# The last matrix product of a retention and MoE kernel: a part of its tokens by Strassen's seven products

## The chip, the cores and the metric

The kernel runs on one core of one Trainium2 chip. Its time is the device time of one execution in microseconds (us), the median of three runs. Before the change it is 807.72 us (807.5 to 809.23).

## The reference

A retention layer (attention with a decay in place of a softmax), then two feed-forward layers, over 4 x 576 = 2304 tokens:

```
ret = (q k^T * scale * decay) v            # 4 batches, 8 heads, 576 positions, 64 wide
h   = ((x w1) * (x w2)) w3 w_out           # 2304 x 512, inner width 1024
g   = max(x w_in, 0) + alpha * min(x w_in, 0)   # 2304 x 2048
out = g w_out2                             # 2304 x 512
```

The change is in the last line alone: `g` (2304 x 2048) times `w_out2` (2048 x 512). The weights come as float64 and are converted on the core.

## The kernel before

Every number is held as the sum of two float32r parts, a high and a low one (`h`, `l`), and each product of two such numbers is three matmuls: h*h, h*l, l*h. ACT makes the high part with a copy, DVE the low part with a subtraction (`split`, lines 172 and 173).

The work goes through stages, most of them bound by TensorE: retention, the two products `a` and `b` (`ab_unit`), the folding of w3 and w_out into one matrix, `y`, and then `g`, which is already made with Strassen's seven products (class `Group`, 3 pairs of token blocks times 8 groups `j` of 256 columns of `g`). Each finished piece of `g` (128 columns of `g` by 384 tokens) is written to DRAM (`keep`, `gd`), since only a part fits on the core.

The output stage (lines 1015 to 1035) reads `g` back. It goes in 48 steps. A step is one `j` (256 rows of `w_out2`, in two chunks of 128) for one block `b` of 384 tokens, and has 3 token tiles x 2 chunks x 3 = 18 matmuls of 128x128 by 128x512, which accumulate in one bank of PSUM for each token tile. The first 16 steps take blocks 0 and 1 by turns for each `j` (6 of the 8 banks); the other 32 take one block after the other. `load_g(n + 3)` loads a step's `g` three steps ahead, `split_g(n + 1)` splits it one step ahead. `ghl` has two buffers, so ACT's copy for step n + 1 waits until PE has ended step n - 1.

Beside these steps the 16 chunks of `w_out2` are converted from float64 (class `Weights`). One `ws.tick()` moves a pipeline of four stages by one piece: ACT reads the raw bits (lines 93, 94), DVE puts a float32 together with four operations (lines 103 to 108), ACT makes the high part (112), DVE the low part (116). A piece is done four ticks after it began, and all 16 take 19 ticks. Six of these ticks stand in the last pair's groups (from `j >= 2`, line 1000), the others in the first 13 steps. The loads of raw weights have three buffers: SP issues the load of a piece only once DVE's line 106 has freed a buffer, and every load behind it in SP's queue waits too.

PE, ACT and SP run their instructions in the order in which the program makes them. DVE's order is set by the compiler's planner, which takes the instruction that is ready by its own estimate, with the earlier one in the program ahead of the later.

`tmp` holds the working tiles of the conversion: three buffers with the tag "a", two with the tag "b". `wa`, `hold` and `xo` hold split operands; `bank(i, ...)` gives one of the eight PSUM banks.

Of the kernel before, what the change touches and what calls it, by code (L numbers as in the profile page):

```python
# [16 lines left out]
P = 128  # L17
B, H, S, D = 4, 8, 576, 64
NPAIR = H // 2
NT, DM, DF1, DF2 = B * S, 512, 1024, 2048  # L20
# [3 lines left out]
C1 = DF1 // P  # L24
# [3 lines left out]
W = 384  # L28
NB = NT // W
# [3 lines left out]
def _f32(ap):  # L33
    return ap.bitcast(F32)
# [5 lines left out]
class Steps:  # L40
# [97 lines left out]
def retention_moe_kernel(ctx: ExitStack, tc, qk, kv, w_out1, w3t, w12, w_in, w_out2, alpha, c_row, c_pair, out):  # L138
    nc = tc.nc

    def pool(stack, name, bufs=1, **kw):
        return stack.enter_context(tc.tile_pool(name=name, bufs=bufs, **kw))
# [4 lines left out]
    raws = pool(ctx, "raws", bufs=3, side="left")  # L147
    tmp = pool(ctx, "tmp", bufs=2, side="left")
# [34 lines left out]
    wac, wo, w3p, wpc, wic, wbc = {}, {}, {}, {}, {}, {}  # L183
# [453 lines left out]
    xo = pool(ctx, "xo", bufs=8, side="left", reuse_waits="tile")  # L637
# [109 lines left out]
    def x_operands(p):  # L747

        x = xs_of[p]
        src = {"B11": x[:, 0:2, 0], "B21": x[:, 2:4, 0], "B22": x[:, 2:4, 1]}  # L750
        b12 = x[:, 0:2, 1]
        room_of = lambda m: a_sum(f"t{p}_{m}")[:, :2 * W].rearrange("p (k n) -> p k n", k=2)

        def hi(op):
            t = xop[p, op] = xo.tile([P, 2, 2, W], F32R, tag="xo", name=f"x{op}_{p}")
            nc.scalar.copy(t[:, 0], src[op])

        def lo(op):
# [33 lines left out]
    def x_room(p):  # L792
        xs_of[p] = xs2.tile([P, KT, 2, W], F32, tag="xs", name=f"xs2_{p}")
# [58 lines left out]
    gd = {}  # L852
# [69 lines left out]
            self.from_sum(self.b3, self.u2, 0, 1)  # L922

    NM = W // P
    steps = [(j, b) for j in range(C1) for b in range(2)] + [(j, b) for b in range(2, NB) for j in range(C1)]
    loaded, ready, accs = {}, {}, {}

    def load_g(n):
        if n < len(steps):
            j, b = steps[n]  # L930
            t = loaded[n] = gr.tile([P, 2, W], F32, tag="gr", name=f"gr{n}")
            for m in range(2):
                nc.sync.dma_start(out=t[:, m], in_=gd[2 * j + m, b])

    def split_g(n):
        if n < len(steps):
            x = loaded.pop(n)
            ready[n] = tuple(ghl.tile([P, 2, W], F32R, tag=f"g{m}", name=f"g{m}{n}") for m in "hl")
# [14 lines left out]
    def some_of(steps, n):  # L953
        for _ in range(min(n, len(steps))):
            steps.pop(0)()

    for n, (p, j) in enumerate(groups):
        last, first = j == C1 - 1 and p + 1 < NP, j == 0 and p > 0
        g = Group(p, j, n)
        flush()  # L960
        g.p1()
        g.p5()
        if last:
            some_of(make, 1)
# [12 lines left out]
        if before:  # L977
            before.p4()
            if first:
                some_of(make, 2)  # L980
                if p + 1 < NP:
                    x_room(p + 1)
                    for o in range(KT):
                        for t in range(2):
                            nc.sync.dma_start(out=xs_of[p + 1][:, o, t], in_=x2d[2 * (p + 1) + t, o])
                else:
                    pt.close()
                    gr = pool(ctx, "gr", side="left", bufs=3, reuse_waits="tile")
# [23 lines left out]
    flush()  # L1012


    pg.close()
    used = 0
    for n, (j, b) in enumerate(steps):
        if ws.at[3] < len(ws.pieces):
            ws.tick()
            ws.until(n_in + 2 * j + 2)  # L1020
        load_g(n + 3)
        split_g(n + 1)
        if b not in accs:
            accs[b] = [bank((used + i) % 8, f"o{b}_{i}") for i in range(NM)]
            used += NM
        h, l = ready.pop(n)
        for i in range(NM):
            ic = slice(i * P, (i + 1) * P)
            for m in range(2):
                wh, wl = wbc[2 * j + m]  # L1030
                for q, (x, y) in enumerate(((h, wh), (h, wl), (l, wh))):
                    nc.tensor.matmul(accs[b][i], x[:, m, ic], y, start=(j == 0 and m == 0 and q == 0),  # L1032
                                     stop=(j == C1 - 1 and m == 1 and q == 2))
            if j == C1 - 1:
                write(b, i)


# [79 lines left out]
```

## Time and profile before

| what | us |
|---|---|
| median of three runs | 807.72 |
| the profiled execution's own time | 808.39 |
| its span, first to last instruction | 806.6 |
| PE busy in the span | 788.3 |
| first matmul of the output stage starts | 604.41 |
| last matmul of the output stage starts | 802.40 |

The profiled execution is 0.67 us above the median, and 1.79 us of it lie outside the span. Matmuls are pipelined: one takes some 0.39 us from its start to its modelled end, and the next starts well before that. The cost of a matmul in a full stream is therefore the distance between two starts, and the same goes for DVE and ACT, where an instruction that needs nothing of the one before it starts a little ahead of its end.

### The profile page before, as it was taken

Reading aid. Unit: us, or ns where it says so; the run is one execution under the profiler, and the core shown is the slowest. Engines: PE = TensorE matmul, PEld = TensorE weight load, DVE = VectorE, ACT = ScalarE, POOL = GpSimd, SP = SyncE. Lnnn points to the kernel's source line nnn. Section 1 sums busy time; section 2 is a strip of 40 time slices with the busy share of each in tenths; the row PEclk is TensorE's granted clock in tenths of the full one; section 3 lists DMA queues with packets and bytes.
Section 4 is the critical chain, followed back from the end, with each engine's and each line's share of the span. In section 5 each row is a group of like instructions: output and inputs, shape, how many; then the busy total and the mean of one; then the engine's idle time right before and its main releaser. Section 6 shows DMA issues by size and latency. Waiting matters only on the chain.

```text
span 806.6 us, 12689 instructions
## 1 busy us (share of the span) xinstructions
PE 788.3 (98%) x4768; PEld 695.3 (86%) x4768; DVE 498.9 (62%) x895; ACT 349.4 (43%) x648; POOL 0.2 (0%) x4
## 2 busy tenths in 40 slices
PE   7889999999999999999999999999999999999998
PEld 4668888888888988999999999999997888888886
DVE  4786686425477689988852578677889923222222
ACT  3452472231245465655534455465566622222121
POOL 0000000000000000000000000000000000000000
PEclk9989999999999999999999999999999999999999
DMA  9833951391166568999925925325557635344341
GB/s 349 312 129 103 330 205 80 105 281 79 55 212 204 183 211 312 304 375 407 394 99 192 363 105 186 118 98 196 177 199 243 220 98 176 105 131 137 98 137 40
DMA packets 80765, 156.24 MB, mean 194 GB/s; under 512 B 9280, under 2 KB 57408, under 8 KB 80704
## 3 DMA queue, kind: packets, MB, share of 16 engines
q1 hardware_dynamic: 80704, 155.43, 55.6%
q8 instruction: 37, 0.61, 0.3%
q14 instruction: 24, 0.20, 0.1%
HBM read 104.02 MB, written 51.38 MB: 193 GB/s over the span
## 4 chain that ended last, share of the span: by engine, by line
PE 91%; DVE 3%; DMA 3%; ACT 2%; issue 1%; SPq 1%; ACTq 0%
PE ps L179 25%; PE o L1032 23%; PE h L871 21%; PE y L804 12%; PE pw L618 5%; PE o L342 2%; PE sc L287 1%; DMA raw<-in_w_dram 1%; DMA kv<-in_kv_dram 1%; PE o L333 1%; PE st L302 1%; DMA gr<-gd 0%; DVE gl L173 0%; DVE xs L349 0%; ACT xh L172 0%
## 5 line engine op out<-in xcount | busy, mean ns | idle before, releaser
L179 PE MATMUL ps<-xh,w 128*128 128x512 f32 (+1 forms) x640 | 187.6, 374 | 2.0 <-ACT w L112 1.8
L1032 PE MATMUL o<-wb,gh 128*128 128x512 f32 x576 | 177.6, 389 | 1.0 <-ACT gh L172 1.0
L179 PEld LDWEIGHTS ps<-xh,w 128*128 128x128 f32 x640 | 117.1, 190 | 23.8 <-ACT w L112 2.0
L1032 PEld LDWEIGHTS o<-wb,gh 128*128 128x128 f32 x576 | 108.0, 188 | 23.7 <-ACT gh L172 1.4
L179 PE MATMUL ps<-xl,w 128*128 128x512 f32 (+1 forms) x320 | 119.0, 372 | 0.0
L1032 PE MATMUL o<-wb,gl 128*128 128x512 f32 x288 | 112.3, 390 | 0.4 <-DVE gl L173 0.4
L173 DVE TENSOR_TENSOR gl<-gr,gh 128x768 fp32r<-128x768 f32 x48 | 46.0, 958 | 99.9 <-ACT gh L172 99.9
L804 PE MATMUL y<-yab,wp 128*128 128x384 f32 x576 | 100.0, 334 | 0.0
L804 PEld LDWEIGHTS y<-yab,wp 128*128 128x128 f32 x576 | 99.9, 188 | 0.1
L172 ACT CAST gh<-gr 128x768 fp32r<-128x768 f32 x48 | 40.2, 838 | 116.4 <-PE o L1032 113.3
L179 PEld LDWEIGHTS ps<-xl,w 128*128 128x128 f32 x320 | 60.9, 190 | 9.9 <-DVE xl L173 0.3
L1032 PEld LDWEIGHTS o<-wb,gl 128*128 128x128 f32 x288 | 54.0, 188 | 12.5 <-DVE gl L173 1.3
L883 DVE SCALAR_TENSOR_TENSOR g<-m,al,g 128x384 f32<-128x384 f32 x48 | 29.7, 618 | 48.9 <-ACT g L882 47.2
L871 PE MATMUL h<-xT,wv 128*128 128x384 f32 x288 | 54.9, 334 | 1.5 <-DVE g L889 1.5
L871 PE MATMUL h<-xT,wu 128*128 128x384 f32 x288 | 55.0, 335 | 0.3 <-ACT h L896 0.3
L871 PEld LDWEIGHTS h<-xT,wv 128*128 128x128 f32 x288 | 50.3, 188 | 1.8 <-DVE g L889 1.8
L108 DVE CUSTOM_DVE_ANT_0 a<-a,b 128x1024 uint16<-128x1024 uint16 x72 | 49.5, 688 | 3.5
L871 PEld LDWEIGHTS h<-xT,wu 128*128 128x128 f32 x288 | 50.2, 188 | 0.9 <-ACT h L896 0.6
L475 ACT CAST ab<-f 128x512 fp32r<-128x512 f32 (+1 forms) x40 | 23.0, 576 | 63.3 <-DVE f L479 54.9
L103 DVE TENSOR_SCALAR a<-a 128x512 f32<-128x512 f32 x72 | 30.4, 422 | 25.6 <-ACT a L93 25.1
L479 DVE TENSOR_TENSOR f<-f,ps 128x512 f32<-128x512 f32 (+1 forms) x40 | 25.3, 632 | 31.5 <-PE ps L179 30.1
L618 PE MATMUL pw<-wo,w 128*128 128x512 f32 x192 | 43.7, 389 | 0.0
(82 smaller groups left out, 1003.0 us busy)
## 6 DMA issues: line engine op xcount, KB each, us to landing
gd<-g SPq DMA_DIRECT2D x96, 192.0 KB, 1.9
gr<-gd SPq DMA_DIRECT2D x96, 192.0 KB, 2.6
abd<-ab SPq DMA_DIRECT2D x32, 512.0 KB, 4.3
raw<-in_w_out_dram SPq DMA_DIRECT2D x24, 512.0 KB, 4.0
yab<-abd SPq DMA_DIRECT2D x24, 384.0 KB, 8.3
raw<-in_w_dram SPq DMA_DIRECT2D x16, 512.0 KB, 7.3
raw<-in_w3t_dram SPq DMA_DIRECT2D x16, 512.0 KB, 4.2
rawi<-in_w_in_dram SPq DMA_DIRECT2D x16, 512.0 KB, 6.2
```

The costliest lines, as they stand in the source:

```text
L103: nc.vector.tensor_scalar(out=a, in0=a, scalar1=self.LEAST, scalar2=self.MOST, op0=ALU.max, op1=ALU.min)
L108: nc.vector.tensor_tensor(out=a.bitcast(I32), in0=a.bitcast(I32), in1=b, op=ALU.add)
L172: nc.scalar.copy(hi, src)
L173: nc.vector.tensor_tensor(out=lo, in0=src, in1=_f32(hi), op=ALU.subtract)
L179: nc.tensor.matmul(ps, a, bb, start=(n == 0), stop=(n == last))
L475: nc.scalar.copy(t[:, 0], f)
L479: nc.vector.tensor_tensor(out=f, in0=f, in1=pss[1], op=ALU.mult)
L618: nc.tensor.matmul(acc[i], a[:, ic], bb, start=(k == 0 and n == 0), stop=(k == C1 - 1 and n == 2))
L804: nc.tensor.matmul(ys[o], wpc[c][a][:, oc], yab[b, c][:, bb], start=(c == 0 and i == 0), stop=(c == C1 - 1 and i == 2))
L871: nc.tensor.matmul(ps, a[:, x, ks], b[:, y, k], start=(fresh and n == 0), stop=(n == 5), skip_group_check=True)
L883: nc.vector.scalar_tensor_tensor(out=g, in0=r, scalar=neg[:, c:c + 1], in1=g, op0=ALU.mult, op1=ALU.add)
L1032: nc.tensor.matmul(accs[b][i], x[:, m, ic], y, start=(j == 0 and m == 0 and q == 0), stop=(j == C1 - 1 and m == 1 and q == 2))
```

## The change

The output stage is cut in two. The first 1024 tokens go as before, but all together: for each `j` the blocks 0 (384 tokens), 1 (384) and 2 (256), which take all eight banks. That makes 24 steps. The other 1280 tokens go in five blocks of 256. For each block and each `j` (40 pieces, called n) a 2x2 product of blocks is made with seven products in place of eight: the tokens' side is cut into A11, A12, A21, A22 (128 rows of `g` by 128 tokens each), the weights' side into B11 to B22 (128 by 256), and with the sums S1 to S4 and T1 to T4 the seven products are added up in halves of four banks. Each product is three matmuls with 256 columns, so a piece has 21 of them.

What has to be made for it: the T sums of the weights for all eight `j` (`t_sums` and its `rest`, two half steps for each `j`), 4/3 of a half step for each plain step once the conversion has ended, and those that are left in one go after the last plain step; for each two pieces eight loads of 128 x 128 (`load_two`) and four additions (`add_two`); for each piece a copy and a subtraction over 7 x 128 columns (`high_part`, `low_part`); and for each block six additions and copies that put the four banks together. The first of these stand in the last six plain steps (`ahead`). The conversion of `w_out2` begins one group later (`j >= 3`), and the pool `back` is closed with the group stage.

```diff
-    back = pool(ctx, "back", side="right", reuse_waits="tile")
     pg = ExitStack()
+    back = pool(pg, "back", side="right", reuse_waits="tile")
...
-    steps = [(j, b) for j in range(C1) for b in range(2)] + [(j, b) for b in range(2, NB) for j in range(C1)]
+    PLAIN = ((0, W), (1, W), (2, 256))
+    steps = [(j, *x) for j in range(C1) for x in PLAIN]
...
-            if j >= 2:
+            if j >= 3:
                 ws.tick()
...
     pg.close()
+    gs = pool(ctx, "gs", side="right", bufs=3, reuse_waits="tile")
+    go = pool(ctx, "go", side="right", bufs=3, reuse_waits="tile")
+    HW = DM // 2
+    T0 = sum(w for _, w in PLAIN)
+    n_tail = (NT - T0) // 256 * C1
+    def t_sums(j):
+        w0, w1 = (tmp.tile([P, DM], F32, tag="a", name=f"w{m}_{j}", bufs=3) for m in range(2))
+        t12 = tmp.tile([P, DM], I32, tag="b", name=f"t12_{j}", bufs=2).bitcast(F32)
...
+        for m, w in enumerate((w0, w1)):
+            h, l = wbc[2 * j + m]
+            nc.vector.tensor_tensor(out=w, in0=_f32(h), in1=_f32(l), op=ALU.add)
+        less(t12[:, :HW], w0[:, HW:], w0[:, :HW])
+        less(t12[:, HW:], w1[:, HW:], t12[:, :HW])
+        def rest():
+            t34 = tmp.tile([P, DM], I32, tag="b", name=f"t34_{j}", bufs=2).bitcast(F32)
+            less(t34[:, :HW], w1[:, HW:], w0[:, HW:])
+            less(t34[:, HW:], w1[:, :HW], t12[:, HW:])
...
+            for t, cols, src in places:
+                nc.scalar.copy(t[:, 0, cols], src)
+            for t, cols, src in places:
+                nc.vector.tensor_tensor(out=t[:, 1, cols], in0=src, in1=_f32(t[:, 0, cols]), op=ALU.subtract)
+        return rest
...
+    def load_two(u):
...
+        for i in range(2):
+            j = (2 * u + i) % C1
+            for m in range(2):
+                for h in range(2):
+                    b, at = divmod(t0 + h * P, W)
+                    nc.sync.dma_start(out=t[:, i, PLACE[f"A{h + 1}{m + 1}"]],
+                                      in_=gd[2 * j + m, b][:, at:at + P])
+    def add_two(u):
...
+        for out, x, y, how in (("S1", "A21", "A22", ALU.add), ("S3", "A11", "A21", ALU.subtract),
+                               ("S2", "S1", "A11", ALU.subtract), ("S4", "A12", "S2", ALU.subtract)):
+            nc.vector.tensor_tensor(out=a[out], in0=a[x], in1=a[y], op=how)
+    def high_part(n):
...
+            nc.scalar.copy(x[:, 0], sums_of[n // 2][:, n % 2])
+    def low_part(n):
...
+            nc.vector.tensor_tensor(out=x[:, 1], in0=sums_of[n // 2][:, n % 2], in1=_f32(x[:, 0]),
+                                    op=ALU.subtract)
+    PRODUCTS = (("A11", "B11", 0, 0), ("S2", "T2", 0, 1), ("S3", "T3", 1, 0), ("S1", "T1", 2, 1), ("A22", "T4", 2, 0),
+                ("A12", "B21", 3, 0), ("S4", "B22", 3, 1))
+    ahead = [lambda: load_two(0), lambda: load_two(1), lambda: (add_two(0), load_two(2)), lambda: high_part(0),
+             lambda: (low_part(0), add_two(1)), lambda: high_part(1)]
+    t_steps = Steps([lambda j=j, m=m: t_rest.pop(j)() if m else t_rest.update({j: t_sums(j)})
+                     for j in range(C1) for m in range(2)])
...
         if ws.at[3] < len(ws.pieces):
             ws.tick()
             ws.until(n_in + 2 * j + 2)
+        else:
+            t_steps.tick(4 / 3)
         load_g(n + 3)
         split_g(n + 1)
+        if n >= len(steps) - len(ahead):
+            ahead.pop(0)()
...
+    t_steps.rest()
+    for n in range(n_tail):
+        j, t0 = n % C1, T0 + n // C1 * 256
+        if j == 0:
+            four = [bank((used + i) % 8, f"q{n}_{i}") for i in range(4)]
+            used += 4
+        high_part(n + 2)
+        low_part(n + 1)
+        if n % 2:
+            add_two(n // 2 + 2)
+            load_two(n // 2 + 3)
+        x = gops.pop(n)
+        for a, op, k, half in PRODUCTS:
+            ps = four[k][:, half * HW:(half + 1) * HW]
...
+            for i, (y, z) in enumerate(((0, 0), (0, 1), (1, 0))):
+                nc.tensor.matmul(ps, a[:, y], b[z], start=(opens and j == 0 and i == 0),
+                                 stop=(j == C1 - 1 and i == 2), skip_group_check=True)
+            if j < C1 - 1:
+                continue
...
+                nc.scalar.copy(e[:, :HW], four[0][:, :HW])
+                nc.vector.tensor_tensor(out=u[:, :HW], in0=e[:, :HW], in1=four[0][:, HW:], op=ALU.add)
...
+            elif op == "B22":
+                nc.vector.tensor_tensor(out=ot[:, :DM], in0=e, in1=four[3], op=ALU.add)
+                nc.sync.dma_start(out=out[t0:t0 + P, :], in_=ot[:, :DM])
```

## Rows read from the trace of the kernel before

**Rows 1.** The page's line of busy us, share of the span and instructions.

```profile
PE 788.3 (98%) x4768; PEld 695.3 (86%) x4768; DVE 498.9 (62%) x895; ACT 349.4 (43%) x648; POOL 0.2 (0%) x4
```

**Rows 2.** Chain of waits that ended last, its last stretches: start us, us, what.

```profile
619.35 183.46 PE o L1032 x808
...
802.83 0.69 DVE ot L946
```

**Rows 3.** Groups by line and form: engine, operation, names, shapes, count, busy, mean ns.

```profile
L1032 PE MATMUL o<-wb,gh 128*128 128x512 f32 x576 | 177.6, 389 | 1.0 <-ACT gh L172 1.0
...
L1032 PEld LDWEIGHTS o<-wb,gh 128*128 128x128 f32 x576 | 108.0, 188 | 23.7 <-ACT gh L172 1.4
...
L179 PE MATMUL ps<-xh,w 128*128 128x256 f32 x128 | 23.2, 283 | 0.0
```

**Rows 4.** Timeline of PE: output stage, then a stretch with 256 columns.

```profile
639.88 0.39 PE L1032 MATMUL o<-wb,gl 128*128 128x512 f32 x1
...
649.40 0.39 PE L1032 MATMUL o<-wb,gl 128*128 128x512 f32 x1
...
260.79 0.28 PE L179 MATMUL ps<-xl,w 128*128 128x256 f32 x1
...
267.63 0.28 PE L179 MATMUL ps<-xl,w 128*128 128x256 f32 x1
```

**Rows 5.** Timeline of DVE, two stretches (start us, us, engine, line, operation).

```profile
362.13 0.42 DVE L714 TENSOR_TENSOR s<-a,a 128x256 f32<-128x256 f32 x1
362.47 0.95 DVE L764 TENSOR_TENSOR t_T<-xs 128x768 f32<-128x768 f32 x1
363.34 0.42 DVE L713 TENSOR_TENSOR s<-s,a 128x256 f32<-128x256 f32 x1
363.79 0.42 DVE L715 TENSOR_TENSOR s<-a,s 128x256 f32<-128x256 f32 x1
...
640.63 0.95 DVE L173 TENSOR_TENSOR gl<-gr,gh 128x768 fp32r<-128x768 f32 x1
641.50 0.68 DVE L116 TENSOR_TENSOR wb<-a,wb 128x512 fp32r<-128x512 f32 x1
642.10 0.42 DVE L103 TENSOR_SCALAR a<-a 128x512 f32<-128x512 f32 x1
...
644.45 0.95 DVE L173 TENSOR_TENSOR gl<-gr,gh 128x768 fp32r<-128x768 f32 x1
```

**Rows 6.** Timeline where the output stage begins: PE, then DVE, then SP.

```profile
602.20 1.32 PE L871 MATMUL h<-xT,wv 128*128 128x384 f32 x6 [1.45 <-DVE g L889]
...
618.36 0.73 PE L1032 MATMUL o<-wb,gh 128*128 128x512 f32 x2 [1.02 <-ACT gh L172]
619.35 0.50 PE L1032 MATMUL o<-wb,gl 128*128 128x512 f32 x1 [0.26 <-DVE gl L173]
...
600.20 0.55 DVE L889 TENSOR_TENSOR g<-h,u 128x384 f32<-128x384 f32 x1
600.66 0.68 DVE L116 TENSOR_TENSOR wb<-a,wb 128x512 fp32r<-128x512 f32 x1
...
601.60 0.55 DVE L889 TENSOR_TENSOR g<-h,p 128x384 f32<-128x384 f32 x1
602.07 0.41 DVE L890 TENSOR_SCALAR m<-g,al 128x384 f32<-128x384 f32 x1
...
613.04 0.90 SPq L933 DMA_DIRECT2D gr<-gd  x2
```

**Rows 7.** Timeline of SP's queue, issues of 128 rows of 512 bytes.

```profile
73.11 1.06 SPq L389 DMA_DIRECT2D per_pair<-const_pair_dram  x2
```

**Rows 8.** DMA issues, all of that line: count, KB each, median us to landing.

```profile
per_pair<-const_pair_dram SPq DMA_DIRECT2D x4, 64.0 KB, 2.1
```

**Rows 9.** Windows: busy us of five engines, then granted clock, DMA share, GB/s.

```profile
44.00:48.00 4.00, 2.74 (x7) 2.06 (x8) 3.69 (x10) 2.36 (x5) 0.00 (x0) 0.50 0.00 0
600.00:610.00 10.00, 8.37 (x40) 6.79 (x39) 10.00 (x21) 6.87 (x13) 0.00 (x0) 1.00 0.61 206
```

More of the change, by code (lines that the diff above doesn't have):

```diff
@@ L929, in load_g @@
         if n < len(steps):
-            j, b = steps[n]
-            t = loaded[n] = gr.tile([P, 2, W], F32, tag="gr", name=f"gr{n}")
+            j, b, w = steps[n]
+            t = loaded[n] = gr.tile([P, 2, W], F32, tag="gr", name=f"gr{n}")[:, :, :w]
             for m in range(2):
-                nc.sync.dma_start(out=t[:, m], in_=gd[2 * j + m, b])
+                nc.sync.dma_start(out=t[:, m], in_=gd[2 * j + m, b][:, :w])
     def split_g(n):
@@ L937, in split_g @@
             x = loaded.pop(n)
-            ready[n] = tuple(ghl.tile([P, 2, W], F32R, tag=f"g{m}", name=f"g{m}{n}") for m in "hl")
+            w = steps[n][2]
+            ready[n] = tuple(ghl.tile([P, 2, W], F32R, tag=f"g{m}", name=f"g{m}{n}")[:, :, :w] for m in "hl")
             split(ready[n][0], ready[n][1], x)
@@ L1015, in retention_moe_kernel, with less @@
     pg.close()
+    gs = pool(ctx, "gs", side="right", bufs=3, reuse_waits="tile")
[3 more added lines that the diff above has]
+    n_tail = (NT - T0) // 256 * C1
+    t123, t4, sums_of, summed, gops = {}, {}, {}, {}, {}
+    def t_sums(j):
+        w0, w1 = (tmp.tile([P, DM], F32, tag="a", name=f"w{m}_{j}", bufs=3) for m in range(2))
+        t12 = tmp.tile([P, DM], I32, tag="b", name=f"t12_{j}", bufs=2).bitcast(F32)
+        def less(out, a, b):
+            nc.vector.tensor_tensor(out=out, in0=a, in1=b, op=ALU.subtract)
+        for m, w in enumerate((w0, w1)):
[7 more added lines that the diff above has]
+            less(t34[:, HW:], w1[:, :HW], t12[:, HW:])
+            t123[j] = xo.tile([P, 2, 2, W], F32R, tag="xo", name=f"t123_{j}").rearrange("p a b w -> p a (b w)")
+            if j % 2 == 0:
+                t4[j // 2] = in_wa(2 + j // 2, f"t4_{j}")
+            at = slice(j % 2 * HW, (j % 2 + 1) * HW)
+            places = ((t123[j], slice(0, DM), t12), (t123[j], slice(DM, DM + HW), t34[:, :HW]),
+                      (t4[j // 2], at, t34[:, HW:]))
+            for t, cols, src in places:
[3 more added lines that the diff above has]
+        return rest
@@ new lines, in b_operand @@
+    def b_operand(j, op):
+        if op[0] == "B":
+            t, at = (wbc[2 * j + int(op[1]) - 1], (int(op[2]) - 1) * HW)
+            return tuple(x[:, at:at + HW] for x in t)
+        t, at = (t4[j // 2], j % 2 * HW) if op == "T4" else (t123[j], (int(op[1]) - 1) * HW)
+        return t[:, 0, at:at + HW], t[:, 1, at:at + HW]
+    A_OPS = ("A11", "A12", "A22", "S1", "S2", "S3", "S4")
+    PLACE = {op: n for n, op in enumerate(A_OPS)} | {"A21": 6}
+    def load_two(u):
+        if 2 * u >= n_tail:
+            return
+        t = sums_of[u] = gs.tile([P, 2, 7, P], F32, tag="gs", name=f"gs{u}")
+        t0 = T0 + 2 * u // C1 * 256
+        for i in range(2):
[5 more added lines that the diff above has]
+                                      in_=gd[2 * j + m, b][:, at:at + P])
@@ new lines, in add_two @@
+    def add_two(u):
+        if 2 * u >= n_tail:
+            return
+        t = sums_of[u]
+        a = {op: t[:, :, n] for op, n in PLACE.items()}
+        for out, x, y, how in (("S1", "A21", "A22", ALU.add), ("S3", "A11", "A21", ALU.subtract),
+                               ("S2", "S1", "A11", ALU.subtract), ("S4", "A12", "S2", ALU.subtract)):
+            nc.vector.tensor_tensor(out=a[out], in0=a[x], in1=a[y], op=how)
+    def high_part(n):
+        if n < n_tail:
+            x = gops[n] = go.tile([P, 2, 7, P], F32R, tag="go", name=f"go{n}")
+            nc.scalar.copy(x[:, 0], sums_of[n // 2][:, n % 2])
@@ L1016, in retention_moe_kernel @@
+    t_steps = Steps([lambda j=j, m=m: t_rest.pop(j)() if m else t_rest.update({j: t_sums(j)})
+                     for j in range(C1) for m in range(2)])
+    t_rest = {}
     used = 0
-    for n, (j, b) in enumerate(steps):
+    for n, (j, b, w) in enumerate(steps):
         if ws.at[3] < len(ws.pieces):
@@ L1020, in retention_moe_kernel @@
             ws.until(n_in + 2 * j + 2)
+        else:
+            t_steps.tick(4 / 3)
         load_g(n + 3)
         split_g(n + 1)
+        if n >= len(steps) - len(ahead):
+            ahead.pop(0)()
         if b not in accs:
-            accs[b] = [bank((used + i) % 8, f"o{b}_{i}") for i in range(NM)]
-            used += NM
+            accs[b] = [bank((used + i) % 8, f"o{b}_{i}") for i in range(w // P)]
+            used += w // P
         h, l = ready.pop(n)
-        for i in range(NM):
+        for i in range(w // P):
             ic = slice(i * P, (i + 1) * P)
@@ L1035, in retention_moe_kernel @@
                 write(b, i)
+    t_steps.rest()
[12 more added lines that the diff above has]
+            ps = four[k][:, half * HW:(half + 1) * HW]
+            a = x[:, :, PLACE[a]]
+            b = b_operand(j, op)
+            opens = op in ("B11", "T3", "T1", "B21")
+            for i, (y, z) in enumerate(((0, 0), (0, 1), (1, 0))):
[3 more added lines that the diff above has]
+                continue
+            if op == "T2":
+                e, u = (tmp.tile([P, DM], F32, tag="a", name=f"{m}{n}", bufs=3) for m in "eu")
+                ot = raws.tile([P, DM], I64, tag="raw", name=f"ot{n}").bitcast(F32)
+                nc.scalar.copy(e[:, :HW], four[0][:, :HW])
+                nc.vector.tensor_tensor(out=u[:, :HW], in0=e[:, :HW], in1=four[0][:, HW:], op=ALU.add)
+            elif op == "T3":
+                nc.vector.tensor_tensor(out=u[:, HW:], in0=u[:, :HW], in1=four[1][:, :HW], op=ALU.add)
+            elif op == "T4":
+                nc.vector.tensor_tensor(out=e[:, HW:], in0=u[:, :HW], in1=four[2][:, HW:], op=ALU.add)
+                nc.vector.tensor_tensor(out=ot[:, DM:].rearrange("p (a w) -> p a w", a=2),
+                                        in0=u[:, HW:].unsqueeze(1).to_broadcast([P, 2, HW]),
+                                        in1=four[2].rearrange("p (a w) -> p a w", a=2), op=ALU.add)
+                nc.sync.dma_start(out=out[t0 + P:t0 + 2 * P, :], in_=ot[:, DM:])
+            elif op == "B22":
+                nc.vector.tensor_tensor(out=ot[:, :DM], in0=e, in1=four[3], op=ALU.add)
+                nc.sync.dma_start(out=out[t0:t0 + P, :], in_=ot[:, :DM])
 _OUTS = [((NT, DM), "float32")]
```

2 lines of the change are left out of this document (added).

## The prediction

> **What bounds the kernel now.** Four views, in this order. First the page's busy line [rows 1]: PE is busy for 98% of the span, DVE for 62%. The reader is to see that only PE's own time can be saved, and that DVE has room on average; what it has in one stage is another matter. Then the chain of waits [rows 2]: from 619.35 us it is one piece of 183.46 us, all of it matmuls of the output stage (line 1032), and behind it one copy on DVE and the last write. So this stage costs what its matmuls cost. Third, the groups by form [rows 3]: all 864 of these matmuls are 512 columns wide, and the trace also has 256 wide ones, the form that the change brings. Last the timelines, for distances from start to start, since one duration (389 ns) overlaps with the next.
>
> A matmul with 512 columns: two starts 14 triples apart lie 9.52 us apart [rows 4], so 9.52 / 42 = 0.2267 us. One with 256 columns: 19 triples in 6.84 us, so 0.120 us, each with a weight load of its own.
>
> **The matmuls.** Removed for 1280 tokens: 10 tiles x 8 j x 6 = 480 of the wide ones, 480 x 0.2267 = 108.8 us. Added: 40 pieces x 21 = 840 narrow ones, 840 x 0.120 = 100.8 us. That is -8.0 us: a seventh of the columns less per product would be 13.6, and the fixed part of 13 ns in each matmul (0.120 against half of 0.2267) takes 5.6 back. The 1024 plain tokens keep 384 matmuls, 87.0 us.
>
> Here a rule speaks against the change. The trace shows 0.120 us from start to start although one weight load lasts 188 ns [rows 3, 4]: loads overlap with matmuls. The Trainium skill ("TensorE: Matmul & The Clock Gate", section "Measured speedup vs the span model") says that a weight load overlaps with matmuls in flight only where the row groups differ, and here all use the whole array. By that rule a narrow matmul would be bound by its load, and the stage would lose instead of win; the trace doesn't agree.
>
> **DVE between the plain steps and the pieces.** This is where I see the price. DVE's cost is the distance between independent starts [rows 5]: 0.34 us for 256 columns, 0.60 for 512, 0.87 for 768, and so 0.87 + 128 x 0.27 / 256 = 1.0 for 896. Where an operation reads the one just before it, 256 columns take 0.45.
>
> The conversion now has 5 ticks in the groups, so its 19th falls on step 13 (counted from 0), and the T sums begin with step 14. From there to the second piece PE has 35.4 us of plain steps (one of 2.72 us and three j of 48 x 0.2267 = 10.88) and 2.5 us of the first piece: 37.9 us. The second piece needs `low_part(1)`. Before that the program gives DVE:
> - T sums: for each j three operations of 512 and six of 256, 3 x 0.60 + 6 x 0.34 = 3.84; for eight j 30.7;
> - nine splits: 6 x 0.87 + 3 x 0.60 = 7.0;
> - `add_two` twice, 8 x 0.34 = 2.7, and `low_part` twice, 2.0;
> - five of the eight copies that empty the plain banks, 5 x 0.60 = 3.0.
>
> That is 45.4 us, 7.5 more than PE has. Upper end: with 0.11 more for each of 16 dependent subtractions 9.3, if all stands in the program's order. Lower end: the three half steps that are left over at the end (1.96 + 3.84 = 5.8 us) are needed by pieces 6 and 7 only; if DVE does them behind `low_part(1)`, and the first half step (1.9) in the light steps 12 and 13, -0.2, so nothing. Which of the two is the planner's choice. The nearest row is the start of the stage [rows 6]: there the planner put a conversion's subtraction (line 116), later in the program, between the last group's additions and what follows from them (lines 889, 890), since those were not ready. The left-over half steps wait too, for ACT's high parts, and ACT, in order, first waits for the last plain bank. So I expect a good part of them behind `low_part(1)`, but not all, and take 3.5 us.
>
> DVE's distances are themselves disputed. The trace shows 256 columns starting 0.34 us after each other with a duration of 0.42 [rows 5]. The Trainium skill ("VectorE: DVE Perf Modes", section "The DRAIN you can't avoid") says that the next operation does not start until the pipeline is empty. By that rule the list costs full durations (0.42, 0.68, 0.95), some 53 us, and PE would wait 15; the trace agrees with the distances, not with this.
>
> **The start of the stage.** Today PE waits for 1.45 us in the last groups, on a DVE addition (line 889) that sits behind a conversion's, and for 1.02 + 0.26 in the fourth step, whose `g` was issued by SP only at 613.04 [rows 6], behind a raw load that waits for DVE. The tick that goes out of group j = 2 leaves DVE's queue as long as it was in the last groups, so I keep these waits. The fourth step now comes after 48 matmuls in place of 54, 1.36 us sooner, while its load does not. Through steps 0 to 13 DVE has a tick of at most 644.45 - 640.63 - 0.87 = 2.95 us [rows 5] in each step and the splits: 3 x 2.95 + 2 x 0.87 + 0.60 = 11.2 for each j, against PE's 10.88. That is 1.5 us over 14 steps, if the tick's dependent operations are not filled in between. Ends: -2.9 (all these waits gone) to +2.9; I take +1.0, near the row of the fourth step.
>
> **The pieces.** A piece takes PE 2.52 us, DVE 1.0 + 2 x 0.34 = 1.7, and ACT one copy of 896 columns, far less than 2.52 even at DVE's price. At a block's end DVE has 3 x 0.34 + 2 x 0.60 = 2.2 us more, 15.8 of 20.2 us in a block. Before the last product DVE has 0.34 + 0.60 in the 0.72 us of two products; the last addition then ends the kernel as the copy does today [rows 2]. I take +0.5 for all five block ends, bounds 0 and 2. SP has eight loads for two pieces, 128 rows of 512 bytes. Today's issues of that form take 1.06 us for two [rows 7], and land after 2.1 us [rows 8]: 8 x 0.53 + 0.23 for the writes = 4.5 of 5.04 us. It holds, with little reserve, and they run two to three pairs ahead. The closed pool and the other buffers cost nothing while these loads stay ahead; if not, it is the SP rival below.
>
> **Sum.** -8.0 + 3.5 + 1.0 + 0.5 = -3.0 us on the profiled execution's 808.39 us (span 806.6 and 1.79 around it), 805.4. That execution is 0.67 above the median, so 804.7 us for the median.
>
> **Rivals.**
> - *DVE's excess falls on PE in full* (slower). The place is the second piece: PE stands idle until T6 and T7 are finished. It costs 9.3 us in place of 3.5: 804.7 + 5.8 = 810.5. If the clock falls to 1.2 GHz in the wait, as in a stretch with PE busy for 2.74 of 4 us [rows 9], 4 us at half speed give back 2: 812.5. For it: the program's order and 45.4 against 37.9. Against it: the planner's habit, and that 1.6 us of idling in 10 left the clock at 1.00 [rows 9]. It decides from an excess of 8.0 - 1.5 = 6.5 us on.
> - *DVE hides it all.* The junction costs nothing and the start neither gains nor loses: -8.0 + 0.5, 800.2 us. For it: the lower end above. Against it: the sum leaves no reserve.
> - *SP's queue becomes the bound.* From 0.60 us an issue on ((5.04 - 0.23) / 8); at 0.70 each pair takes 5.83, 0.8 more, over 17 pairs 13.4 us: about 818. Against it: 0.53 and 0.45 (613.04, two in 0.90 [rows 6]).
> - *A narrow matmul costs its weight load.* 840 x (0.188 - 0.120) = 57 us: 862. Against it: 0.120 over 57 matmuls in a row. The skill's rule on weight loads is the one that would lead here.
> - *DVE costs its full durations*, 15.3 in place of 3.5: 816.5. The skill's rule on the DRAIN is the one.
>
> **How the numbers follow.** Forecast 0.46 (802 to 807.5), excess in full 0.26, all hidden 0.17, SP 0.06, the last two and anything else 0.05. The range runs from 800.0 to 812.5: it takes in the hidden case's middle and the excess with the slow clock, and leaves out about 0.08 below and 0.11 above. The forecast's own range is 802 to 807.5. A change of under 0.2%, 1.6 us, can't be told from none. Faster than that: most of the hidden case and five sixths of the forecast, 0.55; within: 0.12; slower: most of the excess and the rest, 0.33.
>
> **What would show it.** In the profile after: narrow matmuls at line distance 0.120 and 40 x 2.52 us for the pieces; an idle time of PE before the second piece, released by DVE's `low_part`, of 2 to 5 us (8 or more: the rival; none: hidden); DVE near 100% from step 14 to there; the fourth step's wait of 2 to 3 us; SP's loads of the pieces 0.53 apart. I am wrong if PE idles in the middle of the pieces, if the distance isn't 0.120, or if DVE has gaps while PE waits for it.

## The result, and the profile after

The changed kernel takes 814.2 us (median of 4 runs, 813.84 to 815.31), the kernel before 808.48 in the same session (4 runs): ratio 1.0069, 95% interval [1.0055, 1.0083]. It is slower by 0.7%, 5.7 us, clear of the noise. The forecast of 804.7 missed the direction, and 814.2 lies above the range, which ended at 812.5.

The profiled execution took 815.31 us (span 813.5, before 806.6). It is the slowest of the four, 1.1 us above the median, so what is read from it adds up to 6.9 us where the medians differ by 5.7. The page's busy line of the kernel after stands against [rows 1]:

```profile
PE 787.2 (97%) x5128; PEld 710.2 (87%) x5128; DVE 581.0 (71%) x1081; ACT 373.0 (46%) x690; POOL 0.2 (0%) x4
```

PE's busy time is nearly the same while the span is 6.9 us longer: PE waits more. (Its busy sum also hides most of the 8 us saved, in part because a half clock stretches matmuls, below.) DVE has 82 us more work. The waits of PE from 600 us on (who waited, for whom: us in total, times, longest):

```profile
PE q L1154 <- ACT go L1094: 4.1, 1, 4.1
PE q L1154 <- DVE go L1099: 3.7, 5, 1.7
PE o L1131 <- ACT gh L172: 2.5, 1, 2.5
PE h L871 <- DVE g L889: 1.5, 1, 1.5
PE o L1131 <- DVE gl L173: 0.4, 2, 0.3
```

The last three lines also stood before, where the longest were 1.02, 1.45 and 0.26 us [rows 6]; the first two are new, 7.8 us in the pieces. PE's timeline after shows where (start us, us, engine, line, operation, in brackets the idle time ahead and its releaser):

```profile
617.19 0.73 PE L1131 MATMUL o<-wb,gh 128*128 128x512 f32 x2 [2.51 <-ACT gh L172]
618.18 0.80 PE L1131 MATMUL o<-wb,gl 128*128 128x512 f32 x1 [0.26 <-DVE gl L173]
...
622.12 0.62 PE L1131 MATMUL o<-wb,gh 128*128 128x512 f32 x2
...
660.70 0.62 PE L1131 MATMUL o<-wb,gh 128*128 128x512 f32 x2
...
696.06 0.52 PE L1154 MATMUL q<-wb,go 128*128 128x256 f32 x3
...
699.72 0.38 PE L1154 MATMUL q<-wb,go 128*128 128x256 f32 x1 [0.75 <-DVE go L1099]
...
706.30 0.50 PE L1154 MATMUL q<-wb,go 128*128 128x256 f32 x2 [4.05 <-ACT go L1094]
708.51 0.58 PE L1154 MATMUL q<-wb,go 128*128 128x256 f32 x1 [1.70 <-DVE go L1099]
708.88 2.77 PE L1154 MATMUL q<-t,go 128*128 128x256 f32 x12
711.45 2.12 PE L1154 MATMUL q<-wb,go 128*128 128x256 f32 x9
...
714.93 1.24 PE L1154 MATMUL q<-wb,go 128*128 128x256 f32 x9
...
803.33 1.24 PE L1154 MATMUL q<-wb,go 128*128 128x256 f32 x9
804.41 1.60 PE L1154 MATMUL q<-t,go 128*128 128x256 f32 x12
805.85 1.24 PE L1154 MATMUL q<-wb,go 128*128 128x256 f32 x9
```

The line at 660.70 opens step 14, the one at 696.06 the pieces. Three things are to be seen. One piece lasts 805.85 - 803.33 = 2.52 us, 0.120 a matmul. The second piece (699.72) waits 0.75 us, and the third waits 4.05 + 1.70. And right behind that, 12 matmuls take 711.45 - 708.88 = 2.57 us where 1.44 is normal: 0.214 us each, at half clock. The windows of the kernel after show the clock (window: PE, PEld, DVE, ACT, POOL busy, then granted clock, DMA share, GB/s); 1.00 is 2.4 GHz, and a mean of 0.84 or 0.82 means that a part of the 10 us ran at 1.2:

```profile
610.00:620.00 10.00, 7.24 (x27) 5.33 (x26) 8.22 (x15) 4.92 (x8) 0.00 (x0) 0.90 0.74 261
620.00:630.00 10.00, 10.00 (x42) 8.16 (x41) 8.87 (x16) 6.58 (x12) 0.00 (x0) 0.92 0.62 202
...
680.00:690.00 10.00, 10.00 (x46) 8.29 (x45) 10.00 (x22) 5.07 (x9) 0.00 (x0) 1.00 0.56 157
690.00:700.00 10.00, 9.25 (x53) 8.00 (x52) 10.00 (x22) 3.26 (x6) 0.00 (x0) 1.00 0.42 159
700.00:710.00 10.00, 4.25 (x28) 3.84 (x28) 9.25 (x21) 5.08 (x9) 0.00 (x0) 0.84 0.34 106
710.00:720.00 10.00, 10.00 (x72) 10.00 (x72) 5.46 (x9) 2.82 (x3) 0.00 (x0) 0.82 0.37 101
```

DVE is at 10.00 from 680 to 700: it is the engine that is late. But the long wait is named after ACT. ACT's timeline, and below it DVE's, of the kernel after:

```profile
660.67 0.84 ACT L172 CAST gh<-gr 128x768 fp32r<-128x768 f32 x1 [3.46 <-PE o L1131]
...
700.96 1.34 ACT L1052 CAST t<-t 128x512 fp32r<-128x512 f32 x3 [2.62 <-DVE t L1033]
704.18 1.23 ACT L1052 CAST t<-t 128x512 fp32r<-128x512 f32 x3 [1.87 <-DVE t L1033]
705.32 2.62 ACT L1094 CAST go<-gs 128x896 fp32r<-128x896 f32 x3
```

```profile
657.25 0.69 DVE L173 TENSOR_TENSOR gl<-gr,gh 128x512 fp32r<-128x512 f32 x1 [0.94 <-ACT gh L172]
661.54 0.96 DVE L173 TENSOR_TENSOR gl<-gr,gh 128x768 fp32r<-128x768 f32 x1 [3.61 <-ACT gh L172]
...
668.13 0.69 DVE L173 TENSOR_TENSOR gl<-gr,gh 128x512 fp32r<-128x512 f32 x1 [0.81 <-ACT gh L172]
...
698.58 1.08 DVE L1099 TENSOR_TENSOR go<-gs,go 128x896 fp32r<-128x896 f32 x1
...
707.37 1.08 DVE L1099 TENSOR_TENSOR go<-gs,go 128x896 fp32r<-128x896 f32 x1
```

The third piece's `high_part` (line 1094) stands in ACT's queue behind the copies of T6 and T7 (line 1052), and these wait 2.62 and 1.87 us for DVE's sums (line 1033). Between `low_part` of the second piece (698.58) and of the third (707.37) DVE does 5.8 us of left-over T work. And DVE, late at 680, had idled 0.94 + 3.61 + 0.81 = 5.4 us at 656 to 668: `gl` of the next step waited for `gh`, and that for PE (ACT's line at 660.67), so for a free buffer of the two.

The difference of the two profiled executions, from distances of starts:

| part | before | after | loss or gain, us |
|---|---|---|---|
| first matmul of the stage at | 604.41 | 603.11 | -1.30 (from the first 51 us of the kernel, not from the change) |
| matmuls without any loss | 195.87 | 87.05 + 100.8 | -8.02 |
| lost in plain steps | 2.35 (whole stage) | 92.95 - 87.05 = 5.90 | +3.55 |
| lost up to the start of the fifth piece (714.93 + 6 x 0.12 = 715.65) | - | 0.75 + 4.05 + 1.70 idle, 3.0 by half clock and by the starts behind the waits | +9.5 |
| lost in the other 36 pieces | - | 2.7 | +2.7 |
| last matmul to the end of the span | 3.97 | 4.41 | +0.45 |
| sum | | | +6.9 |

### The profile page after: what moved, and what is told of

Read it like the earlier page. It is cut to its first block, busy times and chain, and to the rows that moved or that the text cites. A ratio compares the mean times of both kernels' runs of the same rounds, so it can differ in the third digit from the quotient of the medians.

```text
span 813.5 us, 13851 instructions
## 1 busy us (share of the span) xinstructions
PE 787.2 (97%) x5128; PEld 710.2 (87%) x5128; DVE 581.0 (71%) x1081; ACT 373.0 (46%) x690; POOL 0.2 (0%) x4
## 4 chain that ended last, share of the span: by engine, by line
PE 81%; DVE 6%; DMA 5%; SPq 4%; ACT 2%; issue 2%; DVEq 0%; ACTq 0%
PE ps L179 24%; PE h L871 21%; PE y L804 12%; PE o L1131 7%; PE q L1154 6%; PE pw L618 5%; SPq L1079 3%; PE o L342 2%; DMA gr<-gd 2%; PE sc L287 1%; DMA gs<-gd 1%; DMA raw<-in_w_dram 1%; DMA kv<-in_kv_dram 1%; PE o L333 1%; DVE gs L1089 1%
## 5 line engine op out<-in xcount | busy, mean ns | idle before, releaser
L1131 PE MATMUL o<-wb,gh 128*128 128x512 f32 x256 | 80.0, 394 | 2.5 <-ACT gh L172 2.5
L1154 PE MATMUL q<-t,go 128*128 128x256 f32 x480 | 65.4, 287 | 0.0
L1094 ACT CAST go<-gs 128x896 fp32r<-128x896 f32 x40 | 36.3, 939 | 62.0 <-PE q L1154 28.3
L1154 PEld LDWEIGHTS q<-t,go 128*128 128x128 f32 x480 | 61.8, 196 | 0.0
L1154 PE MATMUL q<-wb,go 128*128 128x256 f32 x360 | 53.0, 289 | 7.9 <-ACT go L1094 4.1
L1131 PEld LDWEIGHTS o<-wb,gh 128*128 128x128 f32 x256 | 48.8, 191 | 13.1 <-ACT gh L172 2.9
L1154 PEld LDWEIGHTS q<-wb,go 128*128 128x128 f32 x360 | 47.7, 196 | 9.6 <-DVE go L1099 5.3
L1131 PE MATMUL o<-wb,gl 128*128 128x512 f32 x128 | 51.0, 398 | 0.5 <-DVE gl L173 0.4
L1099 DVE TENSOR_TENSOR go<-gs,go 128x896 fp32r<-128x896 f32 x40 | 43.2, 1087 | 11.3 <-ACT go L1094 11.2
```

Of the source, the lines that this page charges most:

```text
L1094: nc.scalar.copy(x[:, 0], sums_of[n // 2][:, n % 2])
L1099: nc.vector.tensor_tensor(out=x[:, 1], in0=sums_of[n // 2][:, n % 2], in1=_f32(x[:, 0]), op=ALU.subtract)
L1154: nc.tensor.matmul(ps, a[:, y], b[z], start=(opens and j == 0 and i == 0), stop=(j == C1 - 1 and i == 2), skip_group_check=True)
```

## The experiments

"After" is the changed kernel. Times are compared as ratios to the kernel before, run in the same session; its medians were 809.0 (no T sums, spread half steps, old conversion, g's load first in after), 809.89 (one go behind piece 0, g's load first in the kernel before, three edits, ticks 1 to 6), 809.17 (both edits, pieces 1 and 3, GpSimd) and 808.55 us (the three kernels with 3/2). Pieces "cost" what lies from the first narrow matmul to the last one's end: 100.8 us without loss, 113.0 in after.

**No T sums at all.** A ceiling: what do they cost? The kernel leaves them out and multiplies by blocks of the weights in their place, so its output isn't the product.

```diff
+        if op[0] == "T":
+            op = {"T1": "B12", "T2": "B22", "T3": "B12", "T4": "B21"}[op]
...
-            t_steps.tick(4 / 3)
+            pass
...
-    t_steps.rest()
```

> Leaves the T sums out altogether: the products use the blocks of the weights in their place, so this prices the T work alone; matmuls, loads, copies and sums of the pieces stay. Theory A (DVE's excess of T work is the wait at the junction): under 1 us idle at pieces 1 to 3, no slow clock, 803.5 to 806.5. Theory B (SP's queue): the junction still waits 4 us or more, over 811.

Measured 805.95 us, 0.9957 [0.9942, 0.9973]. The pieces take 102.2 us without a wait at the junction. So the T sums cost 1.0069 - 0.9957 = 1.1%, 9 us, more than the narrow matmuls save.

**Left-over T half steps spread over pieces 0, 2 and 4.**

```diff
-    t_steps.rest()
     for n in range(n_tail):
...
+        if n in (0, 2):
+            t_steps.tick(1)
+        elif n == 4:
+            t_steps.rest()
         x = gops.pop(n)
```

> The three half steps of the T sums that are left after the last plain step are issued in pieces 0, 2 and 4, not in one go ahead of piece 0. Theory A (ACT's queue: the left-over T copies stand ahead of the third piece's high part, and wait for DVE): PE's 4.1 us and 1.7 us of idling at the third piece fall under 1.5 together, the clock stays at 1.00 there, and the time falls by 6 to 9 us from 814.2, to 805 to 808. Theory B (SP's queue: the writes of the plain blocks hold the loads of the pieces until 701 us): the idling stays, 813 to 815.

Measured 808.05 us, 0.9987 [0.9972, 1.0002]. No work is left out, and 0.8% (6.6 us) of the 1.1% is back. PE's waits at the junction in this kernel's timeline, all there are, and below them SP's loads of the pieces:

```profile
699.23 0.38 PE L1156 MATMUL q<-wb,go 128*128 128x256 f32 x1 [0.82 <-DVE go L1099]
705.38 0.39 PE L1156 MATMUL q<-wb,go 128*128 128x256 f32 x1 [0.86 <-DVE go L1099]
```

```profile
700.66 15.70 SPq L1079 DMA_DIRECT2D gs<-gd  x27
```

The third piece's wait of 5.75 us is gone, the fourth piece has one of 0.86 us, and the granted clock stays at 1.00 from 680 us on: pieces 103.3 us. (This execution, 805.06 us, is the fastest of the ten.) Three half steps at one place made the junction's loss. SP's queue, theory B, did not: behind the writes of the plain blocks the loads start at 700.66 here and at 701.15 in after, and the third piece waits only there.

**The same work in one go, but behind piece 0's own parts.** Is it the place in ACT's queue or the amount of work?

```diff
-    t_steps.rest()
     for n in range(n_tail):
...
+        if n == 0:
+            t_steps.rest()
         x = gops.pop(n)
```

> The changed kernel with the left-over T half steps in one go as before, but issued behind the parts of piece 0 (the high part of piece 2 and the low part of piece 1) in place of ahead of them. If it is the place in ACT's queue (the high part of piece 2 behind T copies that wait for DVE): the 4.1 us wait at the third piece goes, and what DVE still lacks shows one or two pieces later, at most 3 us in all: 807 to 811. If it is DVE's amount of work alone, wherever it stands: 813 to 815.

Measured 814.34 us, 1.006 [1.0039, 1.0081]: as slow as after. The wait has only moved on, from the third piece to the fourth (0.83 at the second, then 2.98 for ACT and 0.87 for DVE). There the same copies stand in ACT's queue ahead of the fourth piece's `high_part`. So this run does not separate ACT's queue from the amount of DVE's work; what the spreading shows is that the loss goes when the work isn't in one go.

**Conversion at its old place (tick from group 2 again).**

```diff
-            if j >= 3:
+            if j >= 2:
                 ws.tick()
```

> Undoes one part of the change: the conversion begins in group j = 2 again, one tick earlier. If the later conversion is what makes the start of the stage slower: 811 to 812.5, with the fourth step's wait near 1 us again. If it moved nothing (forecast; the wait comes from 48 matmuls ahead of that step in place of 54): the same waits, 813.5 to 815.

Measured 808.38 us, 0.9986 [0.9969, 1.0002]. I expected no gain: a miss. The T sums begin one step sooner, two half steps are left over in place of three, and the junction's waits in this kernel's timeline are 2.6 us and no half clock follows (in this execution, whose mean granted clock of 0.993 is the highest of the ten):

```profile
698.24 0.51 PE L1154 MATMUL q<-wb,go 128*128 128x256 f32 x2 [0.83 <-ACT go L1094]
699.91 0.38 PE L1154 MATMUL q<-wb,go 128*128 128x256 f32 x1 [1.16 <-DVE go L1099]
703.49 0.39 PE L1154 MATMUL q<-wb,go 128*128 128x256 f32 x1 [0.63 <-DVE go L1099]
```

So "conversion a group later" was itself a large part of the damage, by pushing DVE's T work one step (4 us) towards the pieces: they take 106.5 in place of 113.0 us. Another 1.8 us come from the plain steps (91.1 us), where half clock happened not to follow the fourth step's wait.

**T half steps at 3/2 a step.** Ten steps at 3/2 make 15 of the 16 half steps, so one is left over in place of three (the expectation below counts none). Can DVE's idle time at 656 to 668 us take the others?

```diff
-            t_steps.tick(4 / 3)
+            t_steps.tick(3 / 2)
```

> The kernel after with one number changed: in the plain steps a tick of 3/2 T half steps in place of 4/3, so that none of the 16 is left over at the end. Theory (part of VectorE's time is lost earlier, at 656 to 672 us, where it idles 0.94 + 3.61 + 0.81 us because gl of the next step waits for a ghl buffer, and the T work that could fill it is issued a step later): the left-over work, some 5.8 us of VectorE, falls into this idle time; the idle times at the third piece go from 5.75 to under 2 us, and the half clock with them: 805.5 to 808.5 us, 0.995 to 0.999 of the kernel before. Rival (the junction's wait is set by the whole amount of VectorE's work, wherever it is issued): PE waits as long, only for gl in the last plain steps instead of for the pieces: 812 to 815 us.

Measured 810.77 us, 1.0028 [1.0015, 1.0042], between the two. The pieces are cheap now (102.7 us), but PE waits in the last plain step but one, and half clock follows there:

```profile
690.20 0.73 PE L1131 MATMUL o<-wb,gh 128*128 128x512 f32 x2 [0.47 <-ACT gh L172]
693.71 0.50 PE L1131 MATMUL o<-wb,gl 128*128 128x512 f32 x1 [2.77 <-DVE gl L173]
```

DVE's idle time early on stayed (1.14 + 3.60 us): it lies ahead of the steps in which the higher rate issues more, and step 14 begins at 660.68 here. The tick wins half of what the spreading wins (0.41 of 0.82%); the rest of the wait only moved.

**g's load issued ahead of the tick in the plain steps**, in after and in the kernel before (the same edit there).

```diff
+        load_g(n + 3)
         if ws.at[3] < len(ws.pieces):
             ws.tick()
             ws.until(n_in + 2 * j + 2)
         else:
             t_steps.tick(4 / 3)
-        load_g(n + 3)
```

> In each plain step the load of g is issued before the tick of the conversion, so ahead of the raw load on SP. Theory C (the fourth step waits since its load stands behind a raw load that waits for DVE): the 2.5 us and 0.3 us of idling at 617 us fall under 0.5, the slow clock there goes, and the time falls by 2.5 to 4.5 us, to 810 to 811.7. Rival (DVE's backlog sets the start of the stage, whatever the load): the wait stays or moves a step, within 1 us of 814.2.

> The kernel before with one edit, the load of g ahead of the tick. Its 1.28 us of waits in the fourth step should go, as in the changed kernel: 1 to 1.8 us faster than before, 806.7 to 807.5. If there only a smaller step order made that load late: no difference.

After: 811.93 us, 1.0031 [1.0019, 1.0043]; kernel before: 806.19 us, 0.9958 [0.9946, 0.9971]. In after the fourth step's wait of 2.51 + 0.26 us is down to this line, with no half clock behind it, and the plain steps take 88.3 in place of 92.95 us:

```profile
617.15 0.50 PE L1131 MATMUL o<-wb,gl 128*128 128x512 f32 x1 [0.35 <-DVE gl L173]
```

The reason is SP's queue. In after SP issued that load late (SP's timeline of after):

```profile
610.97 0.33 SPq L85 DMA_DIRECT2D raw<-in_w_out_dram  x1
611.36 0.90 SPq L934 DMA_DIRECT2D gr<-gd  x2
```

The raw load, which the tick issues, waits for a buffer that DVE frees, and `gr` stands behind it. The junction kept its 4.05 + 1.35 us here: the two places are separate. The kernel before wins 0.42% by the same line, 3.4 us, more than expected; in the profiled executions 1.8 us of that lie in the output stage (from its first matmul to its last 198.0 us before, 196.2 with the edit). The kernel before with this line is the fairer base for what Strassen's products are worth.

**Both edits together.**

> The kernel after with two edits together: the left-over T half steps spread over pieces 0, 2 and 4, and g's load issued ahead of the tick. Theory (two separate places: DVE's amount of work at the third piece, SP's queue in the fourth step): the gains add up, 0.9987 - 0.0038 = 0.995 of the kernel before, about 804.4 us; the idle times are some 1.7 us at pieces 1 and 2 and under 0.5 in the fourth step, and the granted clock is 1.00 in the plain steps. Rival (one wait that only moves: with an earlier start, DVE has the less time before the pieces, so that what the start gains is lost at the junction): no better than the spreading alone, 806.5 to 808.5 us, with 4 us or more of idle time at pieces 0 to 2.

Measured 804.08 us, 0.9935 [0.992, 0.9951]. The gains add up: the sum was 0.995.

**Three edits** (these two, and the conversion tick from group 2).

> Three edits together on the changed kernel: left-over T half steps spread over pieces 0, 2 and 4; load of g ahead of the tick; conversion from group j = 2. If the waits are separate, each gain stays: plain steps near 88.3 us, pieces near 103 us, so 800 to 802.5. If they are one backlog that only moves: not under 804.

Measured 804.69 us, 0.9944 [0.9925, 0.9963]: no better than the two, so the old conversion adds nothing to them. The pieces take 106.0 us; the two waits of 0.52 and 1.16 us now lie 1.7 us apart, and the granted clock behind them is 0.92 and 0.91.

**Ticks in groups 1 to 6** on top (`if 1 <= j <= 6:` for the tick).

> As the kernel with three edits, but the six ticks in the groups stand at j = 1 to 6, none at j = 7. The wait of 1.45 us in the last groups is released by a DVE addition behind a conversion's operation; without a tick there it should go, and the time fall by 1 to 2 us more, 798.5 to 801. If DVE's backlog at that place has another source, the same as with three edits.

Measured 803.72 us, 0.9931 [0.9907, 0.9954]. The fourth step's wait is gone and the plain steps take 87.08 us, their minimum; the 1.38 us in the groups stays, and the junction has 0.65 + 1.16 us and half clock.

**The two left-over half steps at pieces 1 and 3** in place of 0 and 2 (`if n in (1, 3):`).

> The kernel with the three edits and ticks in groups 1 to 6, with the two single left-over half steps at pieces 1 and 3 in place of 0 and 2. Theory (VectorE's amount before low_part of the second piece): a half step of 1.3 to 1.9 us less stands ahead of it, the idle time of 1.16 us there goes to 0.3 or less, and with it the half clock behind it (granted clock 0.84 from 690 to 700 us): 801 to 802 us, 0.991 of the kernel before. Rival (the planner puts the ready work first wherever it is issued, so the place in the program changes nothing): 803.5 to 804 us, with the same 0.6 and 1.2 us of idle time.

Measured 803.25 us, 0.9923 [0.991, 0.9937]. The wait that was to go is still there (this kernel's timeline):

```profile
695.22 0.50 PE L1156 MATMUL q<-wb,go 128*128 128x256 f32 x2 [0.74 <-ACT go L1094]
696.88 0.39 PE L1156 MATMUL q<-wb,go 128*128 128x256 f32 x1 [1.16 <-DVE go L1099]
```

The rival holds: moving them one piece moves nothing, and 0.9923 can't be told from 0.9931.

**The opening additions of the T sums on GpSimd**, in the kernel with both edits and in the one with ticks 1 to 6.

```diff
-            nc.vector.tensor_tensor(out=w, in0=_f32(h), in1=_f32(l), op=ALU.add)
+            nc.gpsimd.tensor_tensor(out=w, in0=_f32(h), in1=_f32(l), op=ALU.add)
```

> The same two edits, and the 16 additions that open the T sums (128x512 each) issued on GpSimd in place of VectorE. No trace of this case shows such an addition on GpSimd, so its duration is open. Theory (VectorE's amount of work is what PE waits for at the third piece): VectorE has 16 x 0.60 = 9.6 us less before the pieces, its excess is gone, and the 1.7 us of idle time at pieces 1 and 2 go: 802.5 to 803.5 us, 0.993 of the kernel before. Rival (GpSimd is so slow, or holds VectorE up so much, that the T sums come later than now): idle times of 3 us or more at the pieces, 806 us or more.

> The kernel with the three edits and ticks in groups 1 to 6, and the 16 additions that open the T sums on GpSimd. Theory (VectorE's amount of work): the idle times at pieces 0 and 1 (0.65 and 1.16 us) and the half clock behind them go, some 3.5 us: 800.0 to 801.5 us, 0.990 of the kernel before. Rival (GpSimd late, or in VectorE's way): 805 us or more, with idle times at the pieces released by VectorE operations that wait for GpSimd, or with VectorE's operations of longer duration than 0.69 us at 512 columns.

Measured 805.95 us, 0.9964 [0.995, 0.9977], and 806.53 us, 0.9963 [0.9948, 0.9977]: both some 0.3% worse than without. Groups of the first one, the whole run for GpSimd, then 640 to 700 us for DVE (busy us, mean ns of one):

```profile
L1037 POOL TENSOR_TENSOR w<-wb 128x512 f32<-128x512 f32 x16 | 29.4, 1843 | 670.8 <-DVE wb L116 642.6 <-DVE t L1033 28.2
```

```profile
L1033 DVE TENSOR_TENSOR t<-w,t 128x256 f32<-128x256 f32 x13 | 11.2, 864 | 0.1
L173 DVE TENSOR_TENSOR gl<-gr,gh 128x768 fp32r<-128x768 f32 x9 | 10.1, 1125 | 3.6 <-ACT gh L172 3.6
L173 DVE TENSOR_TENSOR gl<-gr,gh 128x512 fp32r<-128x512 f32 x5 | 6.9, 1376 | 1.5 <-ACT gh L172 1.5
```

An addition shows 1.84 us there (spans on GpSimd are rough in this profile), and DVE's own operations beside it are held up: without GpSimd these three groups have means of 416, 953 and 688 ns. DVE has 16 x 0.68 = 10.9 us less to do, and these three groups alone take 13 x 0.448 + 9 x 0.172 + 5 x 0.688 = 10.8 us longer.

**The tick of 3/2 with g's load first, and with everything.**

> The same tick of 3/2, and g's load issued ahead of the tick. Theory: the gains of the two places add up, 0.0038 less than the tick of 3/2 alone, about 804 us, no worse than the spreading of left-over half steps with g's load first (0.9935). Rival (the light start takes VectorE's idle time away, so the T sums find none): 806 us or more, with idle times of over 2 us before or in the first three pieces.

> The fastest kernel so far (g's load first, conversion ticks in groups 1 to 6, left-over half steps at pieces 1 and 3) with the tick of 3/2. Here the T sums begin a step sooner, so all 16 half steps are done two steps before the pieces, and VectorE's last plain steps are free of them. Theory: the idle times at pieces 0 and 1 (0.74 and 1.16 us) and the half clock go, 801 us, 0.990. Rival (the amount of work before the pieces decides): a wait of 2 to 4 us in the plain steps, 803.5 to 806 us.

Measured 806.38 us, 0.9973 [0.9962, 0.9984], and 802.67 us, 0.9917 [0.99, 0.9934]. In the first (one half step is left over, and stands at piece 0) the rival holds: PE waits 0.42 + 2.78 us for `gh` and `gl` ahead of the pieces, so spreading into the pieces (0.9935) is better than more haste. In the second the T sums begin a step sooner, and the last half step falls on the last plain step; the waits are 1.42 + 0.44 us ahead of the pieces and 0.95 in them, and the clock stays at 1.00; it is the fastest measured, but not told apart from the one before it (0.9923). It beats both kernels, and the kernel before with g's load first (0.9958 [0.9946, 0.9971]) by some 0.4%, 3 us of the 8 that the matmuls save. Ticks in groups 1 to 6 weren't tried in the kernel before, so a part of the 3 us may be theirs.

## Why the prediction was wrong

- **The step that failed** is DVE between the plain steps and the pieces: "So I expect a good part of them behind `low_part(1)`, but not all, and take 3.5 us." The planner did put them there, as I argued. What failed is the price of that, nothing, since they "are needed by pieces 6 and 7 only". Behind `low_part(1)` (698.58) DVE did 5.8 us of T work, 1.3 us of a bank's copy and two additions, and waited 0.7 us before `low_part(2)` (707.37), and PE's second piece lasts 2.52 us. So PE waited 0.75 us at the second piece, where I put the 3.5, and 5.75 at the third. With the half clock and the starts behind the waits the junction cost 9.5 us. The rival "DVE's excess falls on PE in full" came true in kind, with 6.5 us of waits (it had 9.3) and a half clock behind them, but not in place.
- I also followed DVE alone: the left-over copies sit in ACT's in-order queue too, ahead of `high_part` of the third piece, and 4.05 of the 5.75 us are put down to it. That the amount in one place made the loss is shown (spread: 6.6 us back; moved as a whole: nothing back). How much of it is ACT's queue and how much DVE's work stays open.
- The account of 45.4 us against 37.9 from step 14 on was no measure of the second piece either. DVE began with the T sums at 646.78, 14 us before PE came to step 14 (660.70), and had done 4.4 us of them by then, against the 1.9 of my lower end. Of the 5.4 us that it idled behind `gl`, bound by two `ghl` buffers, only 1.7 come after 660.70. What the idle time cost by itself is not shown: the tick of 3/2 did not fill it, and a third `ghl` buffer wasn't tried.
- **The tick taken from group 2.** I counted the T sums from step 14 on, as the program issues them, but only as a fact; that undoing it gives 0.8%, 6.7 us, shows that this one line was worth nearly as much as the whole gain of the matmuls.
- **The start**, +1.0 in the sum, was 3.55. The fourth step's wait came as foreseen ("2 to 3 us": 2.77, against 1.28). What failed is that the sum had no term for a half clock behind it; [rows 9], where the clock stayed at 1.00 beside 1.6 us of idling, was no proof. In after ten matmuls from 618.18 to 622.12 take 3.94 us, before the same ten take 2.40 (from 619.35 [rows 6] to the line below), so the half clock cost 1.5 us:

```profile
621.75 0.62 PE L1032 MATMUL o<-wb,gh 128*128 128x512 f32 x2
```

- **The pieces**, +0.5, were 2.7 in the other 36 and 0.45 at the end, of which waits for DVE's `low_part` are 0.23 + 0.45 + 0.57.
- **The matmuls** were right: -8.0 us, 0.120 us each over 840 (13.6 is an eighth of 108.8, not "a seventh of the columns"). The weight load rival is out: a load of the pieces lasts 196 ns, as the page's line below has it, beside 120 ns from matmul to matmul. So the rule behind it in the Trainium skill ("TensorE: Matmul & The Clock Gate", section "The mechanism", where it stands) isn't borne out by the runs here.

```profile
L1154 PEld LDWEIGHTS q<-t,go 128*128 128x128 f32 x480 | 61.8, 196 | 0.0
```

- **SP** held: eight loads of the pieces from 674.50 us on in 3.76 us, 0.47 each (0.53 was taken), landing after 2.0 us [rows 7, 8]. DVE's distances held as well, 0.34 for 256 columns, so the rival of full durations is out.
- The chances: 0.26 for the rival that came, and 0.33 for slower, were too low for a step whose program order alone gave 9.3, and the rival's 812.5 left out what the start and the other pieces lost.

## What to carry to other kernels

When a change gives work to an engine at 62% on average, add up that engine's work in the stage that takes it, and do so from one operand that the next engine needs to the following one: work that is harmless ahead of the first can be late for the second. Left-over work in one go before a change of phase was the dearest here: spread it over the steps behind the change, and look at every in-order queue that it passes. Look for the order of issues, too: one line moved on SP's queue was worth 0.4% by itself, with or without the change.

## What the runs showed of the hardware

- Half clock behind a wait of some 2 us is a matter of luck here, and can cost as much as the change of the wait itself (1.5 us in after). In the profiled executions the fourth step's wait of 2.51 us in after, 1.99 with the spread half steps and 2.08 with the tick of 3/2 was followed by windows of 0.87 to 0.96; the waits of 2.07 (old conversion), 2.15 (one go behind piece 0) and 2.63 us (no T sums) at the same place by 1.00. Waits of 0.65 and 1.16 us 1.7 us apart gave 0.84 once (ticks in groups 1 to 6) and waits of 0.74 and 1.16 gave 1.00 (half steps at pieces 1 and 3). What decides is open.
- The kernel before shows it too, from one execution to the next: of the 23 of its last session, the seven with a mean granted clock of 0.994 took 807.2 to 808.0 us, the five with 0.989 or less 809.4 to 812.2. A trace without half clock is one execution of several, and a difference of 1 to 3 us between two traces needs the medians beside it.
- At half clock a 256 wide matmul takes 0.214 us from start to start against 0.120: 256 columns more cost 0.2267 - 0.120 = 0.107 us at full clock, and 0.214 is twice that, so the fixed 13 ns of a matmul nearly vanish.
- GpSimd beside DVE: an addition of 128x512 shows some 1.84 us on GpSimd (DVE: 0.68), and three groups of DVE's operations grow beside it (means of 416 to 864 ns for 256 columns, 953 to 1125 for 768, 688 to 1376 for 512), while its copies from PSUM (line 948) stay at 677 ns (679 without).
